# Two FFN1 blocks take the ELU's min part from VectorE instead of a relu from ScalarE, and all such parts read a column of ones

## The chip, the cores and the metric

The kernel runs on one core of a Trainium2 chip. The metric is the device time of one execution in microseconds (us). Before the change it is 337.62 us (median of three runs, 337.44 to 337.65).

## What is computed

Causal attention with 16 extra "beacon" keys per batch, and behind it a feed-forward block with an ELU and no bias. In the reference, cut to what matters:

```python
B, H, S, Nb, D = (8, 8, 576, 16, 64)
scores = scale * np.matmul(q, k_all.transpose(0, 1, 3, 2))    # k_all: beacons, then keys
a = np.exp(scores - max); a /= a.sum(-1) + 1e-09
x = np.matmul(a, v_all)                                        # to (4608, 512)
h = x @ w_in                                                   # 512 -> 2048
g = np.where(h > 0.0, h, np.exp(np.minimum(h, 0.0)) - 1.0)
out = g @ w_out                                                # 2048 -> 512
```

## The kernel before

The whole kernel is one hand-written order of steps. Each step is a small function, registered under its name; a long string names the steps with their arguments (S.1.9 calls S with batch 1, group 9), and the instructions of each engine stand in its queue in the order in which the string names them. Nothing reorders them later. Engines wait for each other by semaphores, which follow from the tiles that the steps read and write.

The steps that the text names:

- lq, lv, wi, wo, lk, lt: loads of q and k, of v, of the weights (issued by GpSimd), and the way of q and k through a scratch in DRAM and back transposed (lt, issued by SyncE).
- T.b.p.n: TensorE transposes of q and k of batch b, head pair p; cq or ck copies them from PSUM to SBUF on VectorE or ScalarE; cb puts in the beacon keys (VectorE, line 277).
- S.b.g: scores of one group of columns into a PSUM tile of tag S (line 322). x.b.g: their exp on ScalarE (337). m.b.p.g: the causal mask on VectorE, a product with a 0/1 triangle (342).
- L, W: sums of the exponentials and the products with v (379). n: the reciprocal of the sums as an Ln and an Exp on ScalarE (436, 439). M: the product of the two into the tokens xT, on VectorE (473, 483, 490).
- F.t.i: FFN1, block i of token tile t, into one PSUM bank of 128x512 (513). Tiles 0 and 1 have 256 tokens, the others 512. There are two banks of this kind (tag hps, one pool with two buffers); a new F waits until all readers of the bank that it takes are through.
- The ELU of such a block goes in one of two ways. First way: e.t.i, exp on ScalarE (523); u.t.i, relu on ScalarE (528); k.t.i on VectorE, min(e - 1, relu), which is the ELU (538). Second way: e.t.i on ScalarE; r.t.i on VectorE, min(e, 1) - 1 (545); g.t.i on VectorE, max(h, r), which reads h from the PSUM bank (550). In the first way the bank is free after e and u, in the second after e and g.
- G.t.q.d: FFN2 of tiles 0 and 1 (559), o and s its copy and store. From tile 2 on FFN2 is done by a scheme with fewer multiplications (steps Z, Q, J, lines 580, 634 to 655), and most of the last two tiles' FFN1 too (X, P, K, E, U, V). wt, H: differences of weights for it, on VectorE (580).

The column of ones is the tile ones, [128, 32] in fp16, set to 1.0 at the start (169); L reads it as weights.

Of the kernel before, what the change touches and what calls it, by code (L numbers as in the profile page):

```python
# [12 lines left out]
ALU = mybir.AluOpType  # L13
# [4 lines left out]
def kernel(  # L18
# [11 lines left out]
    nc = tc.nc  # L30
    P = 128
# [88 lines left out]
    def seg_view(t, b, n_):  # L120
        a, e, r = segs(b)[n_]
        m = (e - a) // r
        return t[m * n_:m * (n_ + 1), 0:H * r * D].rearrange("p (h r d) -> p h r d", h=H, r=r)

    def load_qk(b, n_, h0, h1):
        st[b] = stq[b % 2]
        a, e, r = segs(b)[n_]
        for src, dst in ((q, st[b][0]), (k, st[b][1])):
            nc.gpsimd.dma_start(
                out=seg_view(dst, b, n_)[:, h0:h1, :, :].rearrange("p h r d -> p h (r d)"),  # L130
                in_=src[b, h0:h1, a:e, :].rearrange("h (p r) d -> p h (r d)", r=r),
            )
# [29 lines left out]
    for b in range(B):  # L162
        (nc.sync if b % 2 == 0 else nc.scalar).dma_start(
            out=bk32[NB * b:NB * (b + 1), :, :],
# [3 lines left out]
    ones = konst.tile([P, 32], FP16)  # L168
# [86 lines left out]
    @step  # L255
    def T(b, p, n_):
        a, e, r_ = segs(b)[n_]
        m_ = (e - a) // r_
        if b == 0:
            t_ = bank("hps", BF16, "tq")[:, 0:2 * (e - a)].rearrange("c (i s) -> c i s", i=2)  # L260
        else:
            t_ = psum.tile([P, 2, 1024], BF16, tag="S", name="tp")[:, :, 0:e - a]
        tps[b, p, n_] = t_
        for i, src in enumerate(st[b]):
            sv = seg_view(src, b, n_)
            for r in range(r_):
                for h in range(2):
                    nc.tensor.transpose(
                        out=t_[D * h:D * (h + 1), i, m_ * r:m_ * (r + 1)],
                        in_=sv[:, 2 * p + h, r, :],  # L270
                        identity=identb[m_ * n_:m_ * (n_ + 1), m_ * n_:m_ * (n_ + 1)],
                    )
# [227 lines left out]
    hp, eb, rb, gh, ob = {}, {}, {}, {}, {}  # L500
# [41 lines left out]
    @step  # L542
    def r(t, i):
        rb[t, i] = melt.tile([P, 512], FP16, tag="r", name="r")
        nc.vector.tensor_scalar(
            out=rb[t, i], in0=eb[t, i], scalar1=1.0, scalar2=1.0, op0=ALU.min, op1=ALU.subtract)

    @step
    def g(t, i):
# [263 lines left out]
    S.1.6 x.1.6 F.0.4 F.1.7 e.0.4 k.0.0 cq.1.3.0 S.1.11 S.1.7 m.1.1.0 cb.1.3 r.0.4 g.0.4 e.1.7 r.1.7  # L813
    lq.2.0.0.8 G.0.0.0 x.1.7 F.0.5 x.1.11 e.0.5 S.1.12 g.1.7 cb.2.1 m.1.2.0 x.1.12 S.1.0 F.0.7 r.0.5
    G.0.1.0 S.1.8 x.1.0 g.0.5 F.1.5 e.0.7 x.1.8 m.1.3.1 S.1.10 cb.2.0 m.1.1.1 S.1.9 e.1.5 x.1.10
    u.0.7 k.0.7 cb.2.2 lv.1.0.1 wo.1 u.1.5 k.1.5 x.1.9 F.1.0 u.1.0 e.1.0 m.1.0.0 T.2.0.0 cq.2.0.0
    F.0.3 T.2.1.0 cq.2.1.0 T.2.2.0 e.0.3 u.0.3 m.1.2.1 k.0.3 wt.1.0 k.1.1 ck.2.2.0 F.1.4 F.0.6 e.0.6
    S.2.0 S.2.5 x.2.5 x.2.0 r.0.6 m.1.3.0 G.0.0.1 m.1.0.1 g.0.6 G.0.1.1 k.1.0 lv.1.2.3.4 lp.3.0
    lp.3.1 T.2.3.0 e.1.4 ck.2.3.0 L.1.1 n.1.1 F.1.2 r.1.4 u.1.2 e.1.2 M.1.1.0 W.1.1 M.1.1.1 S.2.3
# [126 lines left out]
```

## Time and profile before

| what | us |
|---|---|
| median of the runs | 337.62 |
| the profiled execution, its own time | 336.87 |
| its span, first to last instruction | 335.2 |
| TensorE (PE) busy | 324.5 |
| ScalarE (ACT) busy | 283.1 |
| VectorE (DVE) busy | 277.0 |
| GpSimd (POOL) busy | 87.3 |

PE is the matmuls, PEld the loading of weights, which runs beside them. Matmuls are pipelined, so one that follows another is issued before the first has ended. In the rows of the profile, L545 is line 545 of the kernel; out<-in are the program's names for the tiles, followed by partitions x elements and their types; xN is the number of instructions in the row. In a row in order of time the first two numbers are the start and the duration in us, and the bracket at the end tells how long the engine was idle before it and what ended that. In a row of groups, after the bar stand the busy time in us, the mean duration of one in ns, and after the second bar the idle time of the engine before them. In a row of waits stand who waited, for whom, the total in us, the number of times and the longest. ScalarE and VectorE overlap the end of an instruction with the start of the next by about 0.1 us, so the durations in a row of several don't add up exactly.

Ten blocks take the second way before: 0.1, 0.2, 0.4, 1.7, 0.5, 0.6, 1.4, 2.3, 2.9 and 2.8, the first at 27.8 us and the last at 93.7 us; 110 take the first.

### The profile page before, as it was taken

Reading aid. Unit: us, or ns where it says so; the run is one execution under the profiler, and the core shown is the slowest. Engines: PE = TensorE matmul, PEld = TensorE weight load, DVE = VectorE, ACT = ScalarE, POOL = GpSimd, SP = SyncE. Lnnn points to the kernel's source line nnn. Section 1 sums busy time; section 2 is a strip of 40 time slices with the busy share of each in tenths; the row PEclk is TensorE's granted clock in tenths of the full one; section 3 lists DMA queues with packets and bytes.
Section 4 is the critical chain, followed back from the end, with each engine's and each line's share of the span. In section 5 each row is a group of like instructions: output and inputs, shape, how many; then the busy total and the mean of one; then the engine's idle time right before and its main releaser. Section 6 shows DMA issues by size and latency. Waiting matters only on the chain. (4 is left out here: it accounts for less than half of the span.)

```text
span 335.2 us, 8837 instructions
## 1 busy us (share of the span) xinstructions
PE 324.5 (97%) x3615; PEld 207.8 (62%) x3615; DVE 277.0 (83%) x590; ACT 283.1 (84%) x465; POOL 87.3 (26%) x121
## 2 busy tenths in 40 slices
PE   8989989999999999999999999999999999999995
PEld 3546656454446555657555666556656788788784
DVE  2662867666899999997999799997999999997971
ACT  2989898899999999989898889897988768879651
POOL 8875586540049106500170060000000000000000
PEclk9999999999999999999999999999999999999999
DMA  8999999999939997995199596000210020021022
GB/s 120 155 180 181 179 182 184 149 165 159 125 49 175 180 125 56 178 155 102 34 137 142 104 72 167 3 33 6 91 34 31 2 96 32 12 84 33 32 90 100
DMA packets 127800, 34.65 MB, mean 103 GB/s; under 512 B 110864, under 2 KB 126224, under 8 KB 127760
## 3 DMA queue, kind: packets, MB, share of 16 engines
q0 software_dynamic: 93632, 18.49, 68.1%
q1 hardware_dynamic: 33552, 15.47, 20.9%
q8 instruction: 28, 0.46, 0.6%
q10 hardware_dynamic: 576, 0.13, 0.2%
q14 instruction: 12, 0.10, 0.1%
HBM read 37.22 MB, written 15.34 MB: 157 GB/s over the span
## 5 line engine op out<-in xcount | busy, mean ns | idle before, releaser
L513 PE MATMUL hps<-xT,w_in 128*128 128x512 f16 (+1 forms) x544 | 118.3, 355 | 1.6 <-ACT r L528 1.5
L337 ACT ACTIVATE et<-sc 128x1024 f16<-128x1024 f32 (+2 forms) x114 | 105.0, 979 | 6.4 <-PE sc L322 6.4
L634 PEld LDWEIGHTS <-gt 128*128 128x128 f16 x768 | 74.1, 98 | 18.7 <-issue 2.0
L538 DVE SCALAR_TENSOR_TENSOR gt<-e,r 128x512 f16<-128x512 f32 x110 | 73.1, 683 | 9.4 <-ACT r L528 7.3
L523 ACT ACTIVATE e<-hps 128x512 f32<-128x512 f32 x120 | 72.8, 626 | 7.6 <-PE hps L513 5.9
L513 PEld LDWEIGHTS <-w_in 128*128 128x128 f16 x544 | 49.8, 98 | 44.8 <-issue 7.2
L528 ACT ACTIVATE r<-hps 128x512 f16<-128x512 f32 x110 | 66.3, 626 | 7.4 <-PE hps L513 4.1
L634 PE MATMUL ops<-w_out,gt 128*128 128x256 f16 x368 | 47.9, 273 | 0.4 <-DVE osb L652 0.4
L634 PE MATMUL ops<-wt,gt 128*128 128x256 f16 x352 | 46.8, 273 | 0.1
L142 POOL DMA_DIRECT2D v<-in_v_dram x40 | 36.0, 1022 | 6.7 <-issue 2.5
L342 DVE TENSOR_TENSOR et<-et,triu 128x512 f16<-128x512 f16 (+4 forms) x108 | 31.8, 332 | 2.4 <-ACT et L337 2.4
L580 DVE TENSOR_TENSOR gt<-gt 128x1024 f16<-128x1024 f16 x48 | 32.5, 684 | 0.5
L379 PEld LDWEIGHTS <-v 128*32 128x32 f16 (+1 forms) x800 | 17.1, 96 | 9.7 <-issue 2.4
L395 DVE TENSOR_TENSOR qk<-qk,et 128x672 f16<-128x672 f16 (+2 forms) x60 | 21.6, 369 | 0.8
L379 PE MATMUL ut<-et,v 128*32 128x464 f16 (+3 forms) x560 | 21.0, 296 | 0.0
L473 DVE TENSOR_TENSOR xT<-ut,rl 128x672 f16<-128x672 f32 (+12 forms) x26 | 16.4, 669 | 1.7 <-ACT rl L439 1.1
L655 DVE TENSOR_TENSOR osb<-ops,sm 128x512 f32<-128x512 f32 x23 | 15.7, 683 | 1.5 <-PE ops L634 1.3
L137 POOL DMA_DIRECT2D v<-in_beacon_v_dram x8 | 6.4, 802 | 39.1 <-PE ut L379 39.1
L559 PE MATMUL ops<-w_out,gt 128*128 128x512 f16 x64 | 16.0, 380 | 0.0
L748 DVE SCALAR_TENSOR_TENSOR gt<-e,r 128x512 f16<-128x512 f32 x24 | 15.9, 684 | 0.0
L634 PE MATMUL ops<-w_out,s 128*128 128x256 f16 x112 | 15.2, 273 | 0.0
L719 ACT COPY kst<-hps 128x512 f32<-128x512 f32 x18 | 10.2, 586 | 5.5 <-PE hps L709 5.3
(114 smaller groups left out, 404.9 us busy)
## 6 DMA issues: line engine op xcount, KB each, us to landing
out_dram<-osb SPq DMA_DIRECT2D x35, 256.0 KB, 2.3
v<-in_v_dram POOLq DMA_DIRECT2D x24, 128.0 KB, 6.7
scr<-in_q_dram POOLq DMA_DIRECT2D x5, 576.0 KB, 13.6
scr<-in_k_dram POOLq DMA_DIRECT2D x5, 576.0 KB, 15.6
w_in<-in_moe_w_in_dram POOLq DMA_DIRECT2D x16, 128.0 KB, 7.4
w_out<-in_moe_w_out_dram POOLq DMA_DIRECT2D x4, 512.0 KB, 9.7
v<-in_v_dram POOLq DMA_DIRECT2D x8, 112.0 KB, 9.6
v<-in_v_dram POOLq DMA_DIRECT2D x8, 80.0 KB, 6.1
```

The source lines that it names most:

```text
L142: nc.gpsimd.dma_start(out=vt[b][r0:r0 + n, j, :, :], in_=v[b, :, ilo[j]:ilo[j] + n, :].rearrange("h s d -> s h d"),)
L337: nc.scalar.activation(out=ets[b, d][:, :, a - EC2 * d:e - EC2 * d], in_=sc[b, g][:, :, a - c0:e - c0], func=AFT.Exp, bias=0.0, scale=SCALE)
L342: nc.vector.tensor_tensor(out=o, in0=o, in1=i, op=ALU.mult)
L379: nc.tensor.matmul(out=t[32 * i:32 * (i + 1), a - qa:e - qa], lhsT=ones[0:kc[j], :] if half is None else v16[0:kc[j], j, h, 32 * half:32 * ...
L395: (nc.vector if eng == "v" else nc.gpsimd).tensor_tensor(out=o, in0=t[0:rows, :, a:e] if n == 0 else o, in1=t[0:rows, :, col:col + e - a], ...
L473: nc.vector.tensor_tensor(out=x_tile(k)[:, 2 * g:2 * g + 2, tok - TT * k:to - TT * k], in0=u[:, :, o - qa:o - qa + w], in1=rls[b, g][:, o: ...
L513: nc.tensor.matmul(out=h[:, n_, :], lhsT=w_in16[:, cc, P * fc:P * (fc + 1)], rhs=xt[k][:, cc, a - TT * k:e - TT * k], start=(cc == 0), sto ...
L523: nc.scalar.activation(out=eb[t, i], in_=flat(hp[t, i]), func=AFT.Exp, bias=0.0, scale=1.0)
L528: nc.scalar.activation(out=rb[t, i], in_=flat(hp[t, i]), func=AFT.Relu, bias=0.0, scale=1.0)
L538: nc.vector.scalar_tensor_tensor(out=half(t, i), in0=eb[t, i], scalar=1.0, in1=rb[t, i], op0=ALU.subtract, op1=ALU.min)
L580: (nc.vector if eng == "v" else nc.gpsimd).tensor_tensor(out=o_, in0=a_, in1=b_, op=op_)
L634: nc.tensor.matmul(out=xy[t, n_][qd], lhsT=lw[:, P * qd:P * (qd + 1)], rhs=wt_[:, c, :], start=(first and c == 0 and (qd == 0 or (t, n_) n ...
```

## The change

Two things. The step r is written as a scalar_tensor_tensor: min with the constant 1.0, then the subtraction of a second tensor, which is one column of the tile ones, repeated along the row. What it computes is the same. And the blocks 0.7 and 1.5 go the second way: at the places where the order had u and k for them, it has r and g.

```diff
     def r(t, i):
         rb[t, i] = melt.tile([P, 512], FP16, tag="r", name="r")
-        nc.vector.tensor_scalar(
-            out=rb[t, i], in0=eb[t, i], scalar1=1.0, scalar2=1.0, op0=ALU.min, op1=ALU.subtract)
+        nc.vector.scalar_tensor_tensor(
+            out=rb[t, i], in0=eb[t, i], scalar=1.0, in1=ones[:, 0:1].broadcast_to([P, 512]),
+            op0=ALU.min, op1=ALU.subtract)
...
     G.0.1.0 S.1.8 x.1.0 g.0.5 F.1.5 e.0.7 x.1.8 m.1.3.1 S.1.10 cb.2.0 m.1.1.1 S.1.9 e.1.5 x.1.10
-    u.0.7 k.0.7 cb.2.2 lv.1.0.1 wo.1 u.1.5 k.1.5 x.1.9 F.1.0 u.1.0 e.1.0 m.1.0.0 T.2.0.0 cq.2.0.0
+    r.0.7 g.0.7 cb.2.2 lv.1.0.1 wo.1 r.1.5 g.1.5 x.1.9 F.1.0 u.1.0 e.1.0 m.1.0.0 T.2.0.0 cq.2.0.0
     F.0.3 T.2.1.0 cq.2.1.0 T.2.2.0 e.0.3 u.0.3 m.1.2.1 k.0.3 wt.1.0 k.1.1 ck.2.2.0 F.1.4 F.0.6 e.0.6
```

After it twelve blocks take the second way and 108 the first. The lines behind the step r move down by one.

## The prediction

> **What bounds the kernel now.** I read four views in this order: the page's busy line, the busy time by stretches, the list of waits, and the instructions in order of time around the place that the list names.
>
> ```profile
> span 335.2 us, 8837 instructions
> PE 324.5 (97%) x3615; PEld 207.8 (62%) x3615; DVE 277.0 (83%) x590; ACT 283.1 (84%) x465; POOL 87.3 (26%) x121
> ```
>
> TensorE (PE) is busy for 324.5 of 335.2 us, and the change leaves its instructions as they are. So the end can move by little more than the idle time of TensorE that is taken out or put in. The stretches and the waits say where some of it is:
>
> ```profile
> core 0: us, PE busy (x) PEld busy (x) DVE busy (x) ACT busy (x) POOL busy (x), PEclk, DMA share, GB/s
> 45.00:47.00 2.00, 0.50 (x10) 0.41 (x5) 0.37 (x1) 2.00 (x5) 1.76 (x3) 1.00 1.44 201
> 60.00:80.00 20.00, 19.96 (x192) 9.27 (x192) 11.71 (x27) 18.50 (x30) 8.82 (x6) 1.00 2.15 157
> ```
>
> ```profile
> PE hps L513 <- ACT r L528: 1.5, 1, 1.5
> ```
>
> In 45 to 47 us TensorE works 0.50 us and VectorE (DVE) 0.37, while ScalarE (ACT) is full. It is the one long stall of TensorE after the start-up, 1.5 us, and what ends it is a relu of ScalarE. The instructions there (start, duration, engine, line):
>
> ```profile
> 43.17 0.62 ACT L523 ACTIVATE e<-hps 128x512 f32<-128x512 f32 x1
> 43.21 0.57 DVE L342 TENSOR_TENSOR et<-et,triu 128x512 f16<-128x512 f16 x2
> ...
> 44.60 0.60 ACT L523 ACTIVATE e<-hps 128x512 f32<-128x512 f32 x1
> ...
> 45.09 1.02 ACT L337 ACTIVATE et<-sc 128x1024 f16<-128x1024 f32 x1
> ...
> 45.99 1.10 ACT L528 ACTIVATE r<-hps 128x512 f16<-128x512 f32 x2
> 46.63 0.69 DVE L538 SCALAR_TENSOR_TENSOR gt<-e,r 128x512 f16<-128x512 f32 x1 [2.84 <-ACT r L528]
> 46.65 1.03 PE L513 MATMUL hps<-xT,w_in 128*128 128x256 f16 x8 [1.50 <-ACT r L528]
> ...
> 46.95 1.06 ACT L337 ACTIVATE et<-sc 128x1024 f16<-128x1024 f32 x1
> 47.24 0.16 DVE L277 TENSOR_TENSOR hi<-bkT 128x16 bf16<-128x16 bf16 x1
> ...
> 47.62 0.45 PE L268 MATMUL tp<-identb,qst 96*64 96x96 bf16 x12
> ...
> 47.92 0.42 DVE L342 TENSOR_TENSOR et<-et,triu 128x512 f16<-128x512 f16 x1
> ...
> 48.36 1.36 DVE L281 COPY qk<-tp 128x1152 bf16<-128x1152 bf16 x1
> ...
> 49.77 0.45 PE L268 MATMUL tp<-identb,qst 96*64 96x96 bf16 x12
> ...
> 50.40 1.92 PE L513 MATMUL hps<-xT,w_in 128*128 128x256 f16 x16
> ```
>
> By the order in the schedule, the exp at 43.17 is e.0.7, the one at 44.60 e.1.5, the two relus at 45.99 are u.0.7 and u.1.5, and the matmul group at 46.65 is F.1.0. There are two PSUM banks with the tag hps, held by F.0.7 and F.1.5. F.1.0 can't begin before u.0.7 has read the first, and u.0.7 stands on ScalarE behind e.1.5 and x.1.10. VectorE meanwhile waits 2.84 us.
>
> **The change part by part.** (1) u.0.7 and u.1.5 leave ScalarE: that is the row of 1.10 us for two. (2) For each of them VectorE does r and g (two operations) instead of k (one), at the same places of its queue. (3) All twelve r are scalar_tensor_tensor (STT) on the fp32 tile e and a column of ones, where ten were tensor_scalar. No DMA, no matmul and nothing on GpSimd or the DMA queues is added or moved.
>
> ```profile
> L538 DVE SCALAR_TENSOR_TENSOR gt<-e,r 128x512 f16<-128x512 f32 x110 | 73.1, 683 | 9.4 <-ACT r L528 7.3 <-ACT e L523 1.8
> L342 DVE TENSOR_TENSOR et<-et,triu 128x512 f16<-128x512 f16 x56 | 23.1, 417 | 2.4 <-ACT et L337 2.4
> L550 DVE TENSOR_TENSOR gt<-hps,r 128x512 f16<-128x512 f32 x10 | 6.9, 688 | 0.5
> L545 DVE TENSOR_SCALAR r<-e 128x512 f16<-128x512 f32 x10 | 4.2, 422 | 6.0 <-ACT e L523 6.0
> L692 DVE TENSOR_TENSOR qst<-xT 128x512 f16<-128x512 f16 x4 | 1.7, 417 | 0.0
> ```
>
> The new r has no row. Below it can't be expected to lie under the 422 ns of the r it replaces; above, the nearest row is k (L538), an STT of the same size with an fp32 and an fp16 operand, 683 ns. The operand of ones is one repeated element. A mask that reads its triu operand more than once (L342) takes 417 ns like a subtraction without repeats (L692), so I take 683. Each r costs 683 - 422 = 0.26 us more, ten of them 2.6 us of VectorE. What of that reaches TensorE is decided one by one.
>
> *The first r (r.0.1).*
>
> ```profile
> 27.76 0.43 DVE L545 TENSOR_SCALAR r<-e 128x512 f16<-128x512 f32 x1 [3.49 <-ACT e L523]
> 28.30 0.69 DVE L550 TENSOR_TENSOR gt<-hps,r 128x512 f16<-128x512 f32 x1
> ...
> 29.11 1.05 PE L513 MATMUL hps<-xT,w_in 128*128 128x256 f16 x8
> 30.08 1.26 PE L379 MATMUL lt<-et,ones 128*32 128x320 f16 x40
> ...
> 31.39 0.73 ACT L436 ACTIVATE rl<-lt 128x640 f32<-128x640 f32 x1
> ...
> 32.92 1.68 DVE L490 TENSOR_TENSOR xT<-ub,rl 128x512 f16<-128x512 f32 x4 [3.21 <-ACT rl L439]
> ...
> 33.95 0.45 PE L268 MATMUL tp<-identb,qst 96*64 96x96 bf16 x12 [0.47 <-DMA w_in<-in_moe_w_in_dram]
> ```
>
> g.0.1 ends at 28.99 and F.0.2, which takes its bank, begins at 29.11. With 0.26 more it begins at 29.37, the sums L.0.B end at 31.60 instead of 31.34, the Ln begins at 31.62 instead of 31.39, then M.0.B and the transposes at 33.95 follow. The row of the transposes names a DMA; I take M.0.B, whose first half ends shortly before (if it is the DMA, this cost is nothing). Cost: 0.23 us.
>
> *The next four (r.0.2, r.0.4, r.1.7, r.0.5).*
>
> ```profile
> 38.83 0.69 DVE L550 TENSOR_TENSOR gt<-hps,r 128x512 f16<-128x512 f32 x1
> ...
> 39.58 0.97 PEld L513 LDWEIGHTS <-w_in 128*128 128x128 f16 x8
> ...
> 40.87 0.60 ACT L523 ACTIVATE e<-hps 128x512 f32<-128x512 f32 x1
> ...
> 41.50 0.43 DVE L545 TENSOR_SCALAR r<-e 128x512 f16<-128x512 f32 x1 [0.43 <-ACT e L523]
> ```
>
> g.0.4 ends at 39.52 and F.0.5 loads its first weights at 39.58, but its matmuls wait for the group before them anyway until 39.80, so of r.0.4's 0.26 I let 0.08 through. r.0.2 is covered by VectorE's wait for e.0.4, r.1.7 by the 0.43 us before r.0.5. r.0.5 itself delays VectorE by 0.26. So the masks of m.1.1.1, which end at 43.21 + 0.57 = 43.78, end at 43.78 + 0.23 + 0.08 + 0.26 = 44.35.
>
> *The stall.* e.0.7 ends at 43.17 + 0.62 + 0.31 = 44.10, so r.0.7 is free to run at 44.35. It ends at 45.03, g.0.7 at about 45.79 (0.07 to its start, 0.69). F.1.0 begins 0.11 later, as F.0.2 did behind g.0.1: 45.90 against 46.65, a gain of 0.75 us. With all early r hidden it would be 45.35 (gain 1.30); with 5 x 0.26 = 1.30 in full it would be 46.65 again (gain 0). These are the bounds of this part; I keep 0.75.
>
> *What is queued behind.* VectorE has cb.2.2, r.1.5, g.1.5, the mask m.1.0.0 and the copy cq.2.0.0 behind it: 45.9 for r.1.5, 46.65 to 47.34 for g.1.5, mask to 47.7, so the copy at 47.65 against 48.36, 0.7 earlier. The transposes at 49.77 (they want the copied bank) and F.1.4 at 50.40 follow it by 0.7. ScalarE keeps up: without the two relus x.1.9 begins at about 46.3 instead of 46.95. VectorE's slack from 43.8 to 46.63 is what hides the new work; gone, each of r.1.5 and g.1.5 would cost its 0.7.
>
> *The later r.* r.0.6 and r.1.4 add 0.52 to VectorE before
>
> ```profile
> 57.79 0.39 DVE L473 TENSOR_TENSOR xT<-lt,rl 128x224 f16<-128x224 f32 x1 [1.48 <-ACT rl L439]
> ```
>
> where it waits 1.48 us, and the last three stand where VectorE is busy for 11.71 of 20 us (60 to 80 above). I cost them at nothing; uncovered they are 5 x 0.26 = 1.3.
>
> **Sum.** -0.75 us, in the span and so in the time. The profiled execution took 336.87 us, 1.67 more than its span; it would take 336.12. The median of the runs is 0.75 above the profiled execution, and I predict from it: 337.62 - 0.75 = 336.87, say 336.9.
>
> **A rule that speaks against it.**
>
> ```profile
> 43.06 0.63 POOL L788 COPY qst<-bkT 128x32 bf16<-128x32 bf16 x1
> ...
> 43.75 0.20 POOL L788 COPY kst<-bkT 128x32 bf16<-128x32 bf16 x1
> ```
>
> The same copy on GpSimd takes 0.63 us beside the masks of m.1.1.1 and 0.20 after them. The Trainium skill (SBUF — State Buffer, "Who interferes with whom") says that a VectorE instruction with two SBUF inputs and a GpSimd instruction that reads SBUF lock each other out, and a one-source VectorE instruction in a two-port mode locks GpSimd out too. The two rows agree with it. An STT r has two such inputs. If these copies come to lie in front of r.0.5 or r.0.7, one of them waits at most 0.63: gain 0.75 - 0.63 = 0.12.
>
> **The rivals.** *More of the gain* (336.3): the early r's cost is taken up by the waits in front of them, gain 1.30. For it: VectorE is idle 3.49 and 0.43 us before two of the five. Against it: F.0.2 starts 0.12 after g.0.1. *The gain is lost at a later gate* (337.6): something that doesn't depend on the early stages holds TensorE up. For it there is
>
> ```profile
> 180.73 0.28 PE L322 MATMUL sc<-kst 64*128 64x256 bf16 x2 [0.54 <-DMA kst<-scr]
> ```
>
> against it that the transfers behind this tile are issued once earlier matmuls let the buffer go, so they move along. *The port* (337.5), as priced above. *Slower* (338.0): VectorE becomes the bound between 27 and 57 us. If the r's extra time reaches TensorE for seven of the ten, 7 x 0.26 = 1.83 stands against the 1.50 of the stall, +0.3; for all ten 2.6, +1.1. It decides where F.1.0 begins later than 46.65, or where the 1.48 at 57.79 is used up: VectorE has 2 x 0.69 + 0.52 = 1.9 more to do between 44 and 57. *The change doesn't do what it says*: the STT takes 422 as well; then the gain is the 1.30 above.
>
> **How the numbers follow.** About 0.2% (0.68 us) can be told from no change here. Forecast, gain 0.4 to 1.1 (336.5 to 337.2): 0.55, of which 0.33 above 0.68 and 0.22 below. More of the gain (STT at 422 with it): 0.17. Later gate: 0.10. Port: 0.02. Slower: 0.16. So faster 0.33 + 0.17 = 0.50; same 0.22 + 0.10 + 0.02 = 0.34; slower 0.16. The range goes from a gain of 1.4, just beyond the upper bound, to a loss of 0.3: 336.2 to 337.9.
>
> **What would show it.** r at L545 as SCALAR_TENSOR_TENSOR of about 683 ns, twelve of them. The wait of F.1.0 at 45 us shrinks from 1.5 to about 0.7 and is ended by VectorE's g, not by ScalarE. F.0.2 begins about 0.25 later, the transposes of 33.95 about 0.2 later, F.1.4 about 0.7 earlier, and from 60 us on the distance stays. Wrong would be: r near 422 or over 900, the transposes at 33.95 unmoved, a DMA that ends TensorE's wait after 60 us, or VectorE without idle time before the row of 57.79.

## The result, and the profile after

| | before | after |
|---|---|---|
| median of ten runs, us | 337.50 | 336.19 |
| lowest to highest, us | 337.10 to 338.78 | 335.55 to 337.15 |
| ratio of the times, 95% interval | | 0.9961 [0.9948, 0.9975] |

The changed kernel is faster by 1.31 us (0.39%; the interval is 0.84 to 1.75 us). The forecast had the sign and the place, but 0.75 us: 336.19 us lies just below its range, whose lower end was 336.2. As a gain, 1.31 us is inside the 1.4 that the range allowed for; before took 337.50 us in this set, 0.12 less than the 337.62 from which the prediction counts.

The page of the changed kernel, its busy line:

```profile
span 335.2 us, 8840 instructions
PE 324.1 (97%) x3615; PEld 207.8 (62%) x3615; DVE 280.7 (84%) x592; ACT 282.2 (84%) x463; POOL 86.8 (26%) x121
```

The span is that of before, and this profiled execution took 336.98 us against 336.87. So this one execution shows no gain, and the first thing to find out is where its gain went. The stretch that was almost empty before, by the busy times by stretches (columns as before):

```profile
45.00:47.00 2.00, 1.68 (x23) 1.23 (x21) 1.90 (x4) 2.00 (x4) 1.91 (x3) 1.00 1.42 198
60.00:80.00 20.00, 19.96 (x196) 9.28 (x192) 12.18 (x27) 18.64 (x29) 8.83 (x6) 1.00 2.15 159
```

TensorE works 1.68 of the 2 us (0.50 before), VectorE 1.90 (0.37 before). The instructions there and at the start, in order of time:

```profile
28.53 0.69 DVE L545 SCALAR_TENSOR_TENSOR r<-e,ones 128x512 f16<-128x512 f32 x1 [3.49 <-ACT e L523]
29.33 0.69 DVE L551 TENSOR_TENSOR gt<-hps,r 128x512 f16<-128x512 f32 x1
30.07 1.03 PE L513 MATMUL hps<-xT,w_in 128*128 128x256 f16 x8
...
33.84 1.68 DVE L490 TENSOR_TENSOR xT<-ub,rl 128x512 f16<-128x512 f32 x4 [3.11 <-ACT rl L439]
34.88 0.45 PE L268 MATMUL tp<-identb,qst 96*64 96x96 bf16 x12 [0.44 <-DMA w_in<-in_moe_w_in_dram]
...
44.44 0.56 DVE L342 TENSOR_TENSOR et<-et,triu 128x512 f16<-128x512 f16 x2
44.92 0.68 DVE L545 SCALAR_TENSOR_TENSOR r<-e,ones 128x512 f16<-128x512 f32 x1
45.71 0.69 DVE L551 TENSOR_TENSOR gt<-hps,r 128x512 f16<-128x512 f32 x1
46.39 0.69 DVE L545 SCALAR_TENSOR_TENSOR r<-e,ones 128x512 f16<-128x512 f32 x1
46.45 1.03 PE L513 MATMUL hps<-xT,w_in 128*128 128x256 f16 x8 [0.33 <-DVE gt L551]
47.18 0.69 DVE L551 TENSOR_TENSOR gt<-hps,r 128x512 f16<-128x512 f32 x1
...
50.20 1.92 PE L513 MATMUL hps<-xT,w_in 128*128 128x256 f16 x16
```

The chain is the one that the prediction laid out: masks, r.0.7, g.0.7, F.1.0. The wait is 0.33 us instead of 1.50, and VectorE's g ends it. But the first r of this execution already begins at 28.53 instead of 27.76, and no changed instruction stands ahead of it. So 0.77 us was lost before the change could act.

To part the change from such differences, I took the start of the same instruction in every kernel, less its start in the profile of before, and how much that shift grew from one mark to the next. The marks are exps of ScalarE (L337) that begin at 27.68, 36.67, 43.65, 53.00, 172.82 and 186.72 us in before, and two of VectorE's additions into osb, at 267.06 and 281.21. Minus is a gain, in us:

| kernel | up to 27.7 | to 36.7 | to 43.7 | to 53.0 (the stall) | to 172.8 | to 186.7 | 267.1 to 281.2 |
|---|---|---|---|---|---|---|---|
| after | +0.76 | +0.16 | +0.05 | -1.18 | 0.00 | +0.63 | -0.31 |
| again | +0.22 | +0.16 | +0.04 | -1.11 | -0.01 | +0.10 | -0.31 |
| order_alone | +0.24 | 0.00 | 0.00 | -1.46 | -0.01 | +0.46 | -0.31 |
| order_again | 0.00 | 0.00 | 0.00 | -1.46 | +0.11 | +0.25 | -0.31 |
| stt_alone | -0.29 | +0.16 | +0.04 | 0.00 | -0.01 | +0.14 | 0.00 |
| one_block | -0.02 | +0.16 | +0.04 | -0.88 | +0.07 | +0.44 | -0.31 |
| stt_moved_only | +0.04 | 0.00 | +0.22 | -1.29 | +0.08 | +0.35 | -0.31 |
| two_memsets | -0.24 | 0.00 | 0.00 | 0.00 | +0.40 | +0.24 | -0.31 |
| first_r_old | -0.29 | +0.45 | +0.27 | -1.17 | +0.42 | +0.12 | -0.31 |
| hybrid | 0.00 | +1.11 | +0.04 | -1.46 | +0.02 | +0.60 | -0.31 |
| keys_early | -0.16 | +0.46 | +1.12 | -1.46 | +0.21 | -0.72 | -0.31 |
| pool_busy_ts | -0.31 | 0.00 | 0.00 | -1.46 | -0.01 | +0.28 | -0.31 |
| pool_busy_stt | +0.04 | +2.01 | +0.04 | -1.10 | 0.00 | +0.22 | -0.31 |

The lower rows are the experiments; "again" is the changed kernel once more. Two columns differ between executions of one and the same kernel: the start-up (+0.76 and +0.22) and the stretch up to 186.7 (+0.63 and +0.10). By less, the stretch up to 172.8 does so too (order_alone -0.01, order_again +0.11, which are one kernel), and four executions lose time ahead of the stall in gaps that the last section deals with. The stretch up to 186.7 holds the wait for the transposed keys (tile kst, score matmuls near 180 us). Its line in the list of waits is, for after:

```profile
PE sc L322 <- DMA kst<-scr: 1.2, 1, 1.2
```

and for the same kernel again

```profile
PE sc L322 <- DMA kst<-scr: 0.6, 1, 0.6
```

against 0.54 in before. The columns that repeat are the change's: +0.16 and +0.05 lost ahead of the stall, -1.18 at it, and -0.31 near 276 us, where nothing was edited. Their sum is -1.28 (after) and -1.22 (again), beside the measured -1.31; the columns that vary are left out of these sums.

### The profile page after: what moved, and what is told of

Same layout as the page of the kernel before. It is cut to its first block, busy times and chain, and to the rows that moved or that the text cites. A ratio compares the mean times of both kernels' runs of the same rounds, so it can differ in the third digit from the quotient of the medians.

```text
span 335.2 us, 8840 instructions
## 1 busy us (share of the span) xinstructions
PE 324.1 (97%) x3615; PEld 207.8 (62%) x3615; DVE 280.7 (84%) x592; ACT 282.2 (84%) x463; POOL 86.8 (26%) x121
## 5 line engine op out<-in xcount | busy, mean ns | idle before, releaser
L337 ACT ACTIVATE et<-sc 128x1024 f16<-128x1024 f32 (+2 forms) x114 | 104.7, 977 | 7.2 <-PE sc L322 7.2
L538 DVE SCALAR_TENSOR_TENSOR gt<-e,r 128x512 f16<-128x512 f32 x108 | 71.8, 684 | 6.7 <-ACT r L528 4.6
L528 ACT ACTIVATE r<-hps 128x512 f16<-128x512 f32 x108 | 65.0, 624 | 7.3 <-PE hps L513 4.1
L749 DVE SCALAR_TENSOR_TENSOR gt<-e,r 128x512 f16<-128x512 f32 x24 | 16.0, 687 | 0.0
```

Source lines behind the costliest of these rows:

```text
L337: nc.scalar.activation(out=ets[b, d][:, :, a - EC2 * d:e - EC2 * d], in_=sc[b, g][:, :, a - c0:e - c0], func=AFT.Exp, bias=0.0, scale=SCALE)
L528: nc.scalar.activation(out=rb[t, i], in_=flat(hp[t, i]), func=AFT.Relu, bias=0.0, scale=1.0)
L538: nc.vector.scalar_tensor_tensor(out=half(t, i), in0=eb[t, i], scalar=1.0, in1=rb[t, i], op0=ALU.subtract, op1=ALU.min)
```

## The experiments

Three questions were open: what the STT costs by itself, what the move of the two blocks brings by itself, and where the 0.31 near 276 us comes from.

**again**, the changed kernel once more, beside the next three.

> The changed kernel once more, beside the others on the same chip. All theories: 1.3 us under the kernel before, as measured (0.84 to 1.75). In its profile the step from 31 us to 50 us is the same as in the first (TensorE 1.1 us earlier at F.1.4 than at r.0.1's time); only the start-up and the wait for the transposed keys near 180 us may differ from one execution to the next.

Measured: 336.39 us against 337.74, ratio 0.9955 [0.9936, 0.9974] (one of its twelve runs took 1823 us, the other eleven 335.19 to 337.9). The result repeats.

**order_alone**: the moved blocks, but every r as before.

```diff
-        nc.vector.scalar_tensor_tensor(
-            out=rb[t, i], in0=eb[t, i], scalar=1.0, in1=ones[:, 0:1].broadcast_to([P, 512]),
-            op0=ALU.min, op1=ALU.subtract)
+        nc.vector.tensor_scalar(
+            out=rb[t, i], in0=eb[t, i], scalar1=1.0, scalar2=1.0, op0=ALU.min, op1=ALU.subtract)
```

> The moved blocks with the old tensor_scalar for all twelve r. Theory 'order': the move is the whole gain and the scalar_tensor_tensor costs some 0.2 to 0.3 us (r.0.1 in front of F.0.2, and the longer r.0.5 and r.0.7 in front of F.1.0), so this kernel is 1.4 to 1.6 us under the kernel before; F.1.0 starts with no wait. Rival 'port': the scalar_tensor_tensor gives part of the gain by letting GpSimd write its descriptors; then this kernel gains less than 1.0.

Measured: 335.42 us, ratio 0.9923 [0.9898, 0.9949], 2.32 us under before, which is more than the 1.4 to 1.6 expected and more than its trace accounts for (1.46 + 0.31 = 1.77); order_again, below, repeats it. Its instructions in order of time:

```profile
44.06 0.43 DVE L545 TENSOR_SCALAR r<-e 128x512 f16<-128x512 f32 x1
...
44.59 0.69 DVE L550 TENSOR_TENSOR gt<-hps,r 128x512 f16<-128x512 f32 x1
44.73 0.67 PE L322 MATMUL sc<-hi 64*128 64x448 bf16 x12
...
45.34 1.04 PE L513 MATMUL hps<-xT,w_in 128*128 128x256 f16 x8
```

F.1.0 follows the scores at 44.73 with no wait: the whole stall is gone (-1.46 in the table). So the move is the gain, and the STT takes some of it back: by the trace 1.46 against 1.18 - 0.16 - 0.05 = 0.97 in after, 0.5 us; by the medians 0.97 us against again, with intervals that just overlap.

**stt_alone**: the other half, all ten r as STT, the order as before.

```diff
-        nc.vector.tensor_scalar(
-            out=rb[t, i], in0=eb[t, i], scalar1=1.0, scalar2=1.0, op0=ALU.min, op1=ALU.subtract)
+        nc.vector.scalar_tensor_tensor(
+            out=rb[t, i], in0=eb[t, i], scalar=1.0, in1=ones[:, 0:1].broadcast_to([P, 512]),
+            op0=ALU.min, op1=ALU.subtract)
```

> The scalar_tensor_tensor for the ten r, and the order of before. Theory 'order': 0.2 to 0.3 us slower than before, F.0.2 and all behind it about 0.2 us later, the stall at F.1.0 still 1.3 to 1.5 us and ended by a relu. Rival 'port': 0.3 us or more faster than before.

Measured: 337.49 us, ratio 0.9994 [0.9972, 1.0017]. The list of waits has the stall as it was:

```profile
PE hps L513 <- ACT r L528: 1.5, 1, 1.5
```

The table gives the STT's cost here as 0.16 + 0.04 and nothing in later stages. The expected loss of 0.2 to 0.3 us doesn't show in the time: the median is 0.25 us under before, and the interval holds a gain as well as a loss of 0.2, so the time decides nothing.

**one_block**: only 0.7 goes the second way.

```diff
-    r.0.7 g.0.7 cb.2.2 lv.1.0.1 wo.1 r.1.5 g.1.5 x.1.9 F.1.0
+    r.0.7 g.0.7 cb.2.2 lv.1.0.1 wo.1 u.1.5 k.1.5 x.1.9 F.1.0
```

> As the changed kernel, but only block 0.7 takes the second way; 1.5 keeps its relu on ScalarE and its k. Theory 'order': the stall of F.1.0 is that of block 0.7's bank alone, so F.1.0 starts as in the changed kernel; F.0.3 then waits for the relu of 1.5, which ends at about 47.2, and VectorE has 0.7 us less to do in front of the copy cq.2.0.0, so the time is within 0.3 us of the changed kernel. Rival: both blocks count for about half of the gain each, then it is 0.6 us slower than the changed kernel.

Measured: 336.52 us, ratio 0.9958 [0.9939, 0.9976], 0.13 us above again and not 0.6 as by the rival; F.1.0 waits 0.33 us for g as in after, and the stall's column is -0.88. The block 0.7 brings most of it, for its bank is the one that F.1.0 takes; 1.5 adds the 0.2 to 0.3 up to -1.11 and -1.18. In one_block VectorE still waits 1.13 us for the relu u.1.5 (ahead of k.1.5 at 46.82).

**two_memsets**: the 0.31 us near 276. In before, VectorE stops for 0.22 us there; in the changed kernel it doesn't. VectorE's instructions in order of time, in before:

```profile
274.89 1.29 DVE L748 SCALAR_TENSOR_TENSOR gt<-e,r 128x512 f16<-128x512 f32 x2
276.40 0.69 DVE L722 TENSOR_TENSOR kst<-hps,kst 128x512 f32<-128x512 f32 x1 [0.22 <-PE ops L634]
```

and in after:

```profile
275.28 1.29 DVE L749 SCALAR_TENSOR_TENSOR gt<-e,r 128x512 f16<-128x512 f32 x2
276.48 0.69 DVE L723 TENSOR_TENSOR kst<-hps,kst 128x512 f32<-128x512 f32 x1
```

From one row to the next it is 1.51 us in before, 1.20 in after. The changed kernel has two more VectorE instructions ahead of this place (r.0.7 and r.1.5); stt_alone has none and shows the stop. The row of before puts the stop down to TensorE; the theory called "stream" says instead that only the place in VectorE's row of instructions counts. To test it, before got two more instructions that do nothing new, and no other edit:

```diff
         nc.vector.memset(ones, 1.0)
+        nc.vector.memset(ones, 1.0)
+        nc.vector.memset(ones, 1.0)
```

> The kernel before with two more memsets of the tile ones right behind the first, at the start, where VectorE then waits 4 us for a load; nothing else differs, so VectorE's instruction stream is longer by two, as it is in the changed kernel. It tests the 0.31 us that all kernels with moved blocks gain between 267 and 281 us. Theory 'stream': in the kernel before, an addition of VectorE at 276.4 us begins 0.3 us after all its inputs are there because of where it stands in VectorE's instruction stream; then this kernel starts that addition without the wait and gains 0.3 us behind 267 us, with the stall at F.1.0 still 1.5 us. Rival 'timing': the 0.31 us comes from the earlier arrival of the moved blocks' work; then nothing changes here (0 us).

Measured: 336.74 us, ratio 0.9987 [0.997, 1.0003]; the time alone decides nothing. Its trace does:

```profile
275.29 1.28 DVE L750 SCALAR_TENSOR_TENSOR gt<-e,r 128x512 f16<-128x512 f32 x2
276.49 0.68 DVE L724 TENSOR_TENSOR kst<-hps,kst 128x512 f32<-128x512 f32 x1
```

The stop is gone (1.20) with the stall at F.1.0 as it was (0.00 in the table). So the 0.31 us belongs neither to the r nor to the ELU's new way, but to the number of instructions ahead; TensorE's work is that of before here. One more is enough: one_block has 591 VectorE instructions against 590 in before and 592 in after, and gains the 0.31 as well. The same execution shows a price at another place (+0.40 up to 172.8), below.

**stt_moved_only**: the STT for 0.7 and 1.5 alone.

```diff
+        if (t, i) in ((0, 7), (1, 5)):
+            nc.vector.scalar_tensor_tensor(
...
+            return
+        nc.vector.tensor_scalar(
...
```

> Blocks 0.7 and 1.5 moved with the scalar_tensor_tensor, the ten old r as tensor_scalar. Theory 'order': the early r's extra time is gone, so the transposes of 33.95 come as in the kernel before (0.17 us sooner than in the changed kernel) and VectorE reaches r.0.7 without delay; only r.0.7's own 0.26 is left: F.1.0 waits about 0.1 us, the step from before 31 us to behind 50 us is 1.25 to 1.45 us (1.46 with no scalar_tensor_tensor, 0.97 with all). Time 1.5 to 1.8 us under the kernel before. Rival: the moved r's own length makes most of the difference to order_alone; then the step is about 1.0 us.

Measured: 335.94 us against 337.27, ratio 0.9953 [0.9933, 0.9974]. The cost of r.0.1 is gone (0.00 to 36.7), 0.22 is lost before 43.7, and the stall gives 1.29. Two expectations were missed: the time is 1.33 us under before, not 1.5 to 1.8, and the step is 1.29 - 0.22 = 1.07, not 1.25 to 1.45. Of the 0.22, 0.17 is a wait of TensorE for the load of w_out (at 39.20), which comes and goes (0.18 in first_r_old, 0.47 in keys_early, none in before or after). At the stall F.1.0 still waits 0.20 us for g, not 0.1: by this one execution the moved r's own length costs some 0.17 of the 0.5 (1.46 - 1.29), and the early r the rest.

**first_r_old**: after, with r.0.1 alone as a tensor_scalar, for the transposes at 33.95, which the profile says wait for a DMA of w_in.

```diff
+        if (t, i) != (0, 1):
+            nc.vector.scalar_tensor_tensor(
...
+            return
+        nc.vector.tensor_scalar(
...
```

> The changed kernel with r.0.1 alone as tensor_scalar. Theory: F.0.2 begins as in the kernel before behind g.0.1, the transposes of 33.95 are not delayed (0.17 us in the changed kernel), all else as in the changed kernel, so the step from before 27 us to behind 50 us is 0.97 + 0.17 = 1.14 us. Rival: the delay of the transposes there comes from the load of w_in that the profile names; then it stays 0.17.

Measured: one execution, 336.38 us. TensorE in order of time:

```profile
33.67 0.45 PE L268 MATMUL tp<-identb,qst 96*64 96x96 bf16 x12 [0.47 <-DMA w_in<-in_moe_w_in_dram]
...
36.15 0.32 PE L268 MATMUL tp<-identb,kst 96*64 96x96 bf16 x5 [0.26 <-issue]
```

The start-up was 0.29 us shorter here, and the transposes moved by the same (33.95 to 33.67). The cost is gone with the one instruction, while the row names the DMA as before: the transposes wait for the chain behind g.0.1 that ends in VectorE's M.0.B, not for the load. All fourteen profiles bear this out: the transposes begin 1.03 or 1.04 us after M.0.B, and after the start of r.0.1 6.19 us in the nine profiles in which it is a tensor_scalar, 6.35 in the five in which it is an STT. The expected step of 1.14 us was missed all the same: this execution has 1.17 - 0.45 - 0.27 = 0.45, for it loses 0.26 us in the second row, a gap in the middle of a run of transposes that no edit touched, and 0.18 waiting for w_out. I come back to the gap in the last section.

**order_again** is order_alone once more, **hybrid** is it with r.2.3 as an STT, **keys_early** is it with the load lk.7.1 moved up to right behind lk.7.0; all three on one chip. The last diff shows the beginning of two long lines.

```diff
+        if (t, i) == (2, 3):
+            nc.vector.scalar_tensor_tensor(
...
```

```diff
-    D.5.1.1 lk.7.0 lp.6.0 Z.4.3.1
+    D.5.1.1 lk.7.0 lk.7.1 lp.6.0 Z.4.3.1
...
-    u.5.9 k.5.9 x.6.0 k.5.12 Z.4.4.0 Z.4.4.1 lk.7.1 F.5.2
+    u.5.9 k.5.9 x.6.0 k.5.12 Z.4.4.0 Z.4.4.1 F.5.2
```

> order_alone once more (moved blocks, all r as tensor_scalar), since its first median, 2.3 us under the kernel before, is more than the 1.46 + 0.31 = 1.77 us that its trace accounts for. Theory 'order': 1.8 us under the kernel before, within 0.5.

> order_alone with r.2.3 alone as scalar_tensor_tensor. In one execution (two_memsets) the tensor_scalar r.2.3 took 1.83 us beside a descriptor-writing instruction of GpSimd, and TensorE waited 0.36 us for its g. Theory 'lock': the scalar_tensor_tensor isn't held up, so this kernel is as fast as order_alone or up to 0.2 us faster in the median, and its runs spread less upwards. Rival 'order' alone: the same as order_alone, as r.2.3 has 1.4 us of waiting of VectorE ahead of it.

> order_alone with the load of the last batch's k into its scratch (lk.7.1) moved in GpSimd's queue from behind lp.6.1 to behind lk.7.0, so that it no longer runs beside the transposing loads of kst near 170 us. In seven profiles those took 10.5 to 11.1 us from issue to landing, and TensorE waited 0.5 to 1.2 us for them near 180 us. Theory: without the load beside them they land in under 8 us, the wait near 180 us is gone, and the kernel is 0.5 to 1.0 us faster than order_alone. Rival: they are slow because of the v loads and by themselves; then nothing changes.

Measured, before on this chip being 337.64: order_again 335.90 us, ratio 0.9951 [0.9934, 0.9968]; hybrid 335.89, 0.9947 [0.9931, 0.9964]; keys_early 335.33, 0.9938 [0.9914, 0.9962]. The move without the STT is worth 1.74 us, the trace says 1.46 + 0.31 = 1.77. hybrid is no better and doesn't spread less. In keys_early TensorE's wait for the keys is absent from the list of waits (0.8 us in order_again), but not by the way expected: the transposing load takes 9.8 us from issue to landing, not under 8 (10.5 to 11.1 in the other kernels). It is 0.57 us below order_again, with overlapping intervals.

**pool_busy_ts** and **pool_busy_stt** put ten GpSimd memsets of a 128x384 tile beside r.2.3, in order_alone and in after.

```diff
-    G.1.1.2 m.3.0.0 lk.4.1 D.3.0.0
+    G.1.1.2 m.3.0.0 pm.10 lk.4.1 D.3.0.0
```

> order_alone with ten memsets of a 128x384 fp16 tile on GpSimd put ahead of lk.4.1, so that GpSimd is at work when VectorE comes to r.2.3 (70 to 71 us). Theory 'lock': the tensor_scalar r.2.3 waits for GpSimd's instruction and takes 0.6 to 2 us instead of 0.42. Rival: the 1.83 us in two_memsets had another cause; r.2.3 takes 0.42 to 0.45 us.

> The changed kernel with the same ten memsets on GpSimd. Theory 'lock' in its narrow form: a scalar_tensor_tensor with two SBUF operands isn't held up by a GpSimd instruction that only writes, r.2.3 takes 0.68 to 0.70 us. Rival: any two-operand instruction of VectorE is held up as well, r.2.3 takes over 0.9 us.

Measured, one execution each: 335.06 and 337.81 us. The tensor_scalar took 533 ns beside them, where the theory expected 0.6 to 2 us and the rival 0.42 to 0.45; the STT took 692, as expected. VectorE and two of the memsets of pool_busy_ts:

```profile
69.07 0.42 POOL L788 MEMSET junk<- 128x384 f16 x1
69.23 0.53 DVE L546 TENSOR_SCALAR r<-e 128x512 f16<-128x512 f32 x1 [1.39 <-ACT e L524]
69.55 0.58 POOL L788 MEMSET junk<- 128x384 f16 x1
```

The r ends 0.27 us after the memset that was at work when it began (69.76 against 69.49). Beside GpSimd's DMA instructions it ends 0.22 to 0.26 after them (last section), so it is held up in the same way here, and by 0.11 us only because a memset takes 0.42. The next memset, which begins while r is at work, takes 0.58. The long time of pool_busy_stt is no effect of the memsets beside r.2.3, which begin at 70.04: 2.01 us of it are lost before 36.7 on the scale of the table, where its trace has

```profile
38.05 0.32 PE L269 MATMUL tp<-identb,kst 96*64 96x96 bf16 x5 [1.66 <-issue]
```

## Why the prediction was right in kind and short in size

The chain of the prediction happened. Two terms of its sum failed: the stall was sized at 0.75 us and gave 0.96, and the stages behind 60 us were put at nothing, without a reason, where they gave 0.31.

- **The duration of the new r: right.** 683 ns from the nearest STT; the profile of after has, by source line (shortest, median and longest in ns, first and last start),

```profile
L545 DVE SCALAR_TENSOR_TENSOR r<-e,ones x12: 678/684/693, 28.5 to 93.5; 128x512 f16<-128x512 f32 x12
```

  The repeated column of ones costs nothing beside a full second tile.
- **r.0.1: right, a little less.** 0.23 said; F.0.2 is 0.20 later (30.07 against 29.11 + 0.76), the transposes 0.17 (34.88 against 33.95 + 0.76). The step from 0.26 to 0.23, between the sums and the Ln, has no source in the prediction; F.0.2 itself came closer behind g.0.1 (0.05 us in after, 0.12 in before). That M.0.B and not the named DMA decides is shown by first_r_old; in again, the same kernel, the list of waits names it itself:

```profile
PE tp L268 <- DVE xT L490: 0.4, 1, 0.4
```

- **The next four: 0.05 reached TensorE**, where 0.08 was let through for r.0.4.
- **The stall: the mechanism right, the term too small.** Said: F.1.0 at 45.90, a gain of 0.75. With the 0.76 of start-up taken off it begins at 46.45 - 0.76 = 45.69, a gain of 0.96. The 0.21 is made of: the masks end at 44.24, not 44.35 (0.11); r begins 0.08 before their recorded end, not at it; g follows r's start by 0.79, not 0.75 (-0.04); F.1.0 follows g's end by 0.05, not 0.11 (0.06). Four small margins, three of them taken on the same side, made a quarter of the term.
- **The bound for a short r: wrong.** With an r of 422 ns the prediction gave 1.30. By its own sum it is more: 43.78 + 0.42 + 0.07 + 0.69 + 0.11 = 45.07, so the whole stall of 1.50 goes. order_alone, with that r, gained 1.46.
- **What is queued behind: right.** F.1.4 moves as F.1.0 does: 50.20 - 0.76 = 49.44, 0.96 before 50.40 (0.7 said, as the stall was sized).
- **The later r: right.** 0.00 from 53 to 172.8 us in after. The wait of 1.48 at 57.79 that covered r.0.6 and r.1.4 is now

```profile
57.59 0.39 DVE L473 TENSOR_TENSOR xT<-lt,rl 128x224 f16<-128x224 f32 x1 [0.96 <-ACT rl L439]
```

- **"From 60 us on the distance stays": wrong.** The step that failed: it had nothing for the 0.31 us near 276 us, which two_memsets shows to come from the number of VectorE's instructions ahead. With the 0.21 above these are 0.52 of the 0.56 us by which the measured 1.31 exceeds the 0.75.
- **The rivals.** "More of the gain" (1.30) met the measured 1.31 in size by luck, for its reason was another: the early r's cost was not taken up, for without the STT the stall's column is -1.46 and nothing is lost ahead of it. "A later gate" fell, though its sign, a DMA that ends a wait of TensorE after 60 us, is there (1.19 us in after, 0.54 in before). The keys' wait takes 0.5 to 1.2 us in all kernels but keys_early, also in stt_alone (0.7), which reached it no earlier, and the load behind it moves with the gain: it is issued at 168.74 in order_again, at 170.10 in before. Whether the gain lengthens the wait by some tenths can't be told from one profile each. "Slower" fell: F.1.0 did not move past 46.65, and VectorE still waits at 57.59. "The port" fell too: the copies on GpSimd took 0.22 and 0.21 us in after, ending at 43.86, before the masks of m.1.1.1.

## What to carry to other kernels

When a TensorE stall is ended by one engine with a full queue while another waits, look at moving that one reader: here it was worth 1.46 of the 1.50 us. Split such a change, since the change of instruction took 0.5 of it back. The version to keep is the order of the change with the old tensor_scalar (335.42 and 335.90 us in two sets), or keys_early (335.33). For differences under 1 us, compare shifts of the same instruction stage by stage over several executions: the span of one profile hid the whole gain.

## What the runs showed of the hardware

**A tensor_scalar can be held up by a GpSimd instruction; an STT wasn't by the DMA instructions.** All ten r of before take 416 to 428 ns. In order_again five of the twelve take 0.56 to 0.80. Two of them, with GpSimd, in order of time:

```profile
39.13 0.89 POOL L142 DMA_DIRECT2D v<-in_v_dram  x1 [2.46 <-issue]
39.44 0.80 DVE L545 TENSOR_SCALAR r<-e 128x512 f16<-128x512 f32 x1
...
41.16 0.73 POOL L142 DMA_DIRECT2D v<-in_v_dram  x1 [1.14 <-DMA qst<-in_q_dram]
41.50 0.62 DVE L545 TENSOR_SCALAR r<-e 128x512 f16<-128x512 f32 x1
```

Each ends 0.22 us (39.13 + 0.89 = 40.02, 40.24) and 0.23 us (41.89, 42.12) after GpSimd's instruction. In two_memsets r.2.3 was caught by one of 2.19 us:

```profile
70.14 2.19 POOL L774 DMA_DIRECT2D scr<-in_k_dram  x1 [2.48 <-issue]
70.76 1.83 DVE L547 TENSOR_SCALAR r<-e 128x512 f16<-128x512 f32 x1 [1.39 <-ACT e L525]
...
73.37 1.90 PE L515 MATMUL hps<-xT,w_in 128*128 128x512 f16 x12 [0.36 <-DVE gt L552]
```

1.41 us longer than alone, and here it reached TensorE: this is most of the +0.40 in the table. The STT isn't touched; r.2.3 beside the same GpSimd instruction in stt_alone, and r.1.7 in after:

```profile
70.75 2.19 POOL L773 DMA_DIRECT2D scr<-in_k_dram  x1 [1.77 <-issue]
70.93 0.69 DVE L545 SCALAR_TENSOR_TENSOR r<-e,ones 128x512 f16<-128x512 f32 x1 [1.39 <-ACT e L523]
...
40.58 0.89 POOL L142 DMA_DIRECT2D v<-in_v_dram  x1 [3.25 <-issue]
40.63 0.68 DVE L545 SCALAR_TENSOR_TENSOR r<-e,ones 128x512 f16<-128x512 f32 x1
```

Every STT r beside a DMA instruction, in all profiles that have one, took 678 to 693 ns. Beside GpSimd's small memsets and copies (43.46 to 44.42 us in pool_busy_stt) one took 766. Nor is a tensor_scalar held up by each overlap: in order_alone one that begins at 34.76, 0.05 us after a DMA instruction, takes 416 ns, and in before one at 53.53 too, inside an instruction recorded from 52.40 to 54.22. What decides isn't shown.

The Trainium skill (SBUF — State Buffer, "Who interferes with whom") says that a tensor_scalar can enter a mode that takes the port pair shared with GpSimd for the whole instruction, and that whoever comes second is blocked; it infers that descriptor generation needs the pair's write side, which an instruction with two SBUF inputs doesn't take. The rows of the held r agree with both, and so do those of the memsets, where r and then the next memset come second; the overlaps without a delay show no such lock. Its warning is of GpSimd being starved; here VectorE is mostly the one that waits. So the STT is a protection that costs 0.26 us each: here the price by the trace (0.5 us) was higher than what it protects from, for the delayed r of order_again cost nothing at TensorE up to 53 us, and an STT for r.2.3 alone brought nothing measurable (hybrid).

**The place in the row of instructions counts.** 0.31 us near 276 us came and went with two more VectorE instructions at the start. The traces show a load of instructions at this place that moves with the count: a packet of 8 KB of the DMA queue q14, which the page lists with the kind instruction, begins 0.81 and 0.67 us after that addition in the two kernels with the stop (before, stt_alone), 0.01 and 0.18 after it in two_memsets and one_block, and 1.3 to 1.7 ahead of it in the other ten. That this load makes the stop is not shown.

**Gaps of TensorE with no work to wait for.** In the middle of the transposes near 36 to 38 us, some executions have gaps that the profile puts to "issue": 0.26 us of idle time in first_r_old, 0.27 in keys_early, 0.93 in hybrid, 1.66 in pool_busy_stt, none in the other ten profiles (keys_early has a second, of 0.40, at 37.66). They go with a late load of instructions. A 16 KB packet of the queue q8, of the kind instruction too, begins 0.22 to 1.29 us ahead of the first transposes (33.95 in before) in the ten profiles without a gap. In keys_early, first_r_old, hybrid and pool_busy_stt it begins 0.14, 0.22, 0.70 and 1.43 us after them, and the gap ends 1.3 to 1.6 us after the packet. So the transposes probably wait for their own instructions; no run moved the packet to test it.
